# Linear attention and a squared-ReLU layer on one core: the second batch's exp of q by tile and head with its sum on ScalarE, scaling and small additions moved, due dates set anew

## The chip, the core and the metric

The kernel runs on one core of a Trainium2 chip. Its engines are TensorE (PE in the rows), which multiplies matrices, VectorE (DVE), ScalarE (ACT), GpSimd (POOL) and SyncE (SP); SP and ACT also issue DMA transfers. PEld is TensorE's loading of weights. Each engine runs its own list of instructions in order and waits at semaphores. The metric is the device time of one execution in microseconds (us), as the median of several runs.

## The reference

```
def _attn_ref(q, k, v):                       # each (8, 8, 576, 64): batch, heads, sequence, head size
    q_s = exp(q - max(q, axis=-1));  q_s = q_s / (sum(q_s, axis=-1) + 1e-09)
    k_s = exp(k - max(k, axis=2));   k_s = k_s / (sum(k_s, axis=2) + 1e-09)
    kv = einsum('bhsd,bhse->bhde', k_s, v)
    return einsum('bhsd,bhde->bhse', q_s, kv)
x = attn_out.transpose(0, 2, 1, 3).reshape(4608, 512)
r = maximum(x @ w_in, 0.0)                    # w_in (512, 2048)
out = (s * (r * r) + b) @ w_out               # w_out (2048, 512)
```

## The kernel before

**The second layer** takes nearly all of TensorE's time. It goes through 9 blocks of 512 rows of x: one for each batch, with the sequence's first 512 rows, and a last one with the 64 rows left of each batch. In a block there are 16 steps, one for each 128 of the 2048 hidden columns; t counts the steps over all blocks. A step computes `h` (12 matmuls: x and the weights are split into a high and a low part, and three of the four products are summed), takes `r` = relu(h) on ScalarE, makes `gh` and `gl`, the high and low part of s*r*r + b, and adds 12 matmuls to `acc`. There is one PSUM buffer for `h`, so the next h waits for the relu. In the first block a step has two forms: with the square on VectorE, or (every odd t) all on ScalarE but the last subtraction; the second is called the long form here.

**The weights** of the 16 steps are fetched in the first block, and converted there (`conv_w`): on ScalarE two passes (L202, L205) and a cast (L223), on VectorE four passes and a subtraction (L225).

**The attention** works on pairs of heads. A tile u holds two heads, a pair pr two such tiles, so each batch has u = 0 to 3 and pr = 0, 1. For u = 0 to 7 (batches 0 and 1) `q_stream` takes the maximum of q over 64 columns, subtracts it, takes the exp on ScalarE, sums, adds 1e-9, takes the reciprocal, multiplies, turns q with five transposes (`qT`), copies it (`early`), and multiplies it by `kvf` into `xp`, which is cast and split into x. `k_stream` does the same along the sequence with the first batch's k: transpose (`kT`), maximum `km`, exp with its sum, transpose back (`kn`), copy. `heads` computes `kv`; `scales` makes the reciprocal z of k's sums and, with the 0/1 mask `own`, the factors `zr`; `blocks` multiplies kv by them into `kvf`, whose blocks off the diagonal are zero. For the second batch `k_pair` and `kv_second` do this while the first block of the layer runs. Later batches have their own functions, which the change does not touch.

**The order** is made before the program: all this work is written as generators of `Op(engine, cost, due, needs, ...)`, and `Order.run` takes at each point the operation that can start first by its costs; of those within NEAR of each other, the one with the earliest due number. DUE_K, DUE_Q, DUE_V and DUE_W are these numbers for k, q, kv and the first weights; AHEAD sets how many steps ahead a weight tile is due. What comes out is a fixed list for each engine. Where TensorE would wait before the first h, transposes of `ident` into an unused buffer are put in (L948).

**Transfers** are issued by SP in the order of `transfers`, q of the first pair by ACT in `others`.

Of the kernel before, what the change touches and what calls it, by code (L numbers as in the profile page):

```python
# [26 lines left out]
def attention_moe(ctx: ExitStack, tc: tile.TileContext, q, k, v, w_in, w_out, s, b, out):  # L27
# [285 lines left out]
    def blocks(pr, kv, zr):
        kvf = kvfs[pr % 2]
        shape = [P, 2, 2, D]
        nc.vector.tensor_tensor(
            out=kvf, in0=kv.unsqueeze(2).to_broadcast(shape), in1=zr.unsqueeze(3).to_broadcast(shape), op=ALU.mult
        )
        return kvf
# [63 lines left out]
    def kv_second(pr):  # L383
# [4 lines left out]
        yield Op("DVE", 0.5, due)  # L388
        zr = scales(pr, small.tile([P, 2], F32, name=f"z_{pr}", tag="z"), kv[:, :, D])
        yield Op("DVE", 0.4, due, free=["sm"], gives=[f"kvf{pr}"])  # L390
        blocks(pr, kv[:, :, 0:D], zr)

    def kv_stream(pr):
        us = (2 * pr, 2 * pr + 1)
        due = DUE_V[pr]
# [7 lines left out]
        yield Op("DVE", 0.4, due, free=["sm"], gives=[f"kvf{pr}"])  # L403
        blocks(pr, kv, zr)

    def q_stream(u):
# [11 lines left out]
        yield Op("ACT", 0.63, due, take=["qe"], gives=[f"qe{u}"])
        qe = work.tile([P, NT, 2, D], F32, name=f"qe_{u}", tag="qe", bufs=2)
        nc.scalar.activation(qe.rearrange("p n h d -> p h n d"), qt, AF.Exp)  # L420
        yield Op("DVE", 0.73, due)
        qs = small.tile([P, NT, 2], F32, name=f"qs_{u}", tag="qs", bufs=2)
        nc.vector.tensor_reduce(out=qs, in_=qe, axis=AX.X, op=ALU.add)  # L423
        yield Op("DVE", 0.2, due)
        nc.vector.tensor_scalar(qs, qs, 1e-9, None, op0=ALU.add)
# [4 lines left out]
        yield Op("PE", 0.6, due, take=[tag, "qf"], free=["qe"])  # L430
        qT = ps.tile([P, 2, 512], F32, name=f"qT_{u}", tag=tag, bufs=bufs).rearrange("p a b -> p (a b)")
        for n in range(NT):
            nc.tensor.transpose(qT[:, n * P:(n + 1) * P], qe[:, n, :, :].rearrange("p h d -> p (h d)"), ident)
# [565 lines left out]
```

## Time and profile before

| | |
|---|---|
| median of 3 runs | 872.88 us (872.28 to 872.96) |
| the profiled execution | 873.09 us, its span 871.1 us |
| TensorE | 854.6 us busy, 98% of the span |
| VectorE | 576.1 us, 66% |
| ScalarE | 411.9 us, 47% |
| GpSimd | 96.0 us, 11% |
| mean granted clock of TensorE | 0.997 of 2.4 GHz |

The span reaches from the first instruction to the last; the execution's own time is 2.0 us longer. The shares of VectorE and ScalarE are means over stages that differ: in the first block both are far busier than later.

### The profile page before, as it was taken

The page shows a single profiled execution, that of the slowest core. Times are in us where ns is not written, and L with a number is a line of the kernel's source. Part 1 is how long each engine was busy: PE and PEld are TensorE (multiplying, and loading weights), DVE is VectorE, ACT ScalarE, POOL GpSimd, SP SyncE. Part 2 cuts the span into 40 slices and gives each one's busy share as a digit, 9 for nine tenths or more (in the row PEclk, how much of TensorE's full clock was granted, in tenths as well). Part 3 has the DMA queues.
Part 4 walks back from the last instruction along what each step waited for, and adds up shares of the span by engine and source line. Part 5 has one row for each costly group of instructions (what it writes and reads, how often), then busy time and mean ns, then how long its engine had stood idle before and what let it go on. Part 6 is the DMA issues. An engine that isn't in the chain of part 4 may idle for free.

```text
span 871.1 us, 11605 instructions
## 1 busy us (share of the span) xinstructions
PE 854.6 (98%) x4369; PEld 703.6 (81%) x4369; DVE 576.1 (66%) x933; ACT 411.9 (47%) x678; POOL 96.0 (11%) x110
## 2 busy tenths in 40 slices
PE   7899999999999999999999999999999999999997
PEld 6677877888888888888888888888888888888886
DVE  7999997596967778686587758685765332232222
ACT  5898854444554545364345444454444322222222
POOL 1001002020202111120021202030110010000000
PEclk9999999999999999999999999999999999999999
DMA  9977034524343334242433242432311000000001
GB/s 240 320 270 236 13 84 117 130 59 112 121 98 88 83 103 114 89 99 71 130 89 82 89 130 61 109 89 78 81 61 52 25 24 1 1 28 21 1 1 48
DMA packets 110119, 79.44 MB, mean 91 GB/s; under 512 B 60656, under 2 KB 103920, under 8 KB 109936
## 3 DMA queue, kind: packets, MB, share of 16 engines
q1 hardware_dynamic: 108576, 77.60, 32.0%
q10 hardware_dynamic: 1488, 1.12, 0.4%
q8 instruction: 34, 0.56, 0.3%
q14 instruction: 21, 0.17, 0.1%
HBM read 60.29 MB, written 18.40 MB: 90 GB/s over the span
## 4 chain that ended last, share of the span: by engine, by line
PE 86%; issue 6%; DVE 5%; ACT 1%; DMA 1%; POOL 0%; ACTq 0%; DVEq 0%
PE acc L822 41%; PE h L729 41%; PE kv L301 2%; PE xp L679 1%; DVE w L225 1%; DVE low L218 1%; PE xq L679 1%; DMA q<-in_q_dram 1%; DVE low L208 0%; DVE st L213 0%; DVE st L215 0%; POOL k L488 0%; PE xp L443 0%; DVE q L417 0%; DVE qs L423 0%
## 5 line engine op out<-in xcount | busy, mean ns | idle before, releaser
L729 PE MATMUL h<-x,w 128*128 128x512 f32 x1728 | 421.9, 392 | 1.9 <-DVE x L452 0.9
L729 PEld LDWEIGHTS h<-x,w 128*128 128x128 f32 x1728 | 323.5, 188 | 71.5 <-ACT r L773 2.0
L822 PE MATMUL acc<-w,gh 128*128 128x512 f32 x1154 | 357.4, 391 | 0.0
L822 PEld LDWEIGHTS acc<-w,gh 128*128 128x128 f32 x1154 | 214.6, 188 | 44.5 <-ACT last L856 0.4
L788 DVE SCALAR_TENSOR_TENSOR r<-r,sb 128x512 f32<-128x512 f32 x135 | 104.6, 775 | 191.3 <-ACT r L773 190.9
L822 PE MATMUL acc<-w,gl 128*128 128x512 f32 x577 | 224.9, 390 | 0.4 <-DVE gl L785 0.4
L773 ACT ACTIVATE r<-h 128x512 f32<-128x512 f32 x143 | 85.4, 597 | 287.0 <-PE h L729 278.6
L792 DVE SCALAR_TENSOR_TENSOR gl<-r,sb,gh 128x512 fp32r<-128x512 f32 x135 | 107.8, 799 | 53.4 <-ACT gh L790 52.4
L790 ACT ACTIVATE gh<-r,sb 128x512 fp32r<-128x512 f32 x135 | 97.8, 724 | 75.8 <-DVE r L788 75.3
L822 PEld LDWEIGHTS acc<-w,gl 128*128 128x128 f32 x577 | 108.3, 188 | 24.6 <-DVE gl L785 1.6
L578 POOL TENSOR_TENSOR q<-q,qm 128x640 f32<-128x640 f32 x24 | 34.7, 1448 | 174.1 <-DVE qm L576 174.1
L595 POOL TENSOR_TENSOR qe<-qe,qr 128x640 f32<-128x640 f32 x24 | 34.4, 1437 | 58.1 <-DVE qr L591 36.9
L685 ACT COPY y<-xp 64x320 f32<-64x320 f32 x48 | 20.2, 420 | 13.7 <-PE xp L679 13.0
L689 DVE TENSOR_TENSOR y<-xp,y 64x320 f32<-64x320 f32 x48 | 23.5, 489 | 1.5 <-ACT y L685 0.4
L301 PEld LDWEIGHTS kv<-v,k 128*64 128x64 f32 x600 | 18.8, 137 | 6.6 <-issue 4.8
L565 ACT ACTIVATE k<-k 128x640 f32<-128x640 f32 x24 | 17.6, 737 | 13.1 <-DVE k L527 10.3
L659 POOL TENSOR_TENSOR spare<-kvf,spare 128x256 fp32r<-128x256 f32 x12 | 9.7, 808 | 123.1 <-issue 116.1
L301 PE MATMUL kv<-v,k 128*64 128x65 f32 (+1 forms) x600 | 21.0, 224 | 1.3 <-POOL k L488 1.3
L697 DVE TENSOR_TENSOR x<-y,x 128x512 fp32r<-128x512 f32 x24 | 22.3, 931 | 0.0
L599 DVE STREAM_TRANSPOSE q<-qe 128x640 f32<-128x640 f32 x24 | 20.0, 833 | 2.3 <-POOL qe L595 2.3
L616 DVE TENSOR_TENSOR qhl<-qT,qhl 64x640 fp32r<-64x640 f32 x24 | 19.8, 823 | 2.4 <-ACT qhl L611 1.7
L582 ACT ACTIVATE qe<-q 128x640 f32<-128x640 f32 x24 | 18.9, 788 | 5.0 <-POOL q L578 4.8
(126 smaller groups left out, 621.7 us busy)
## 6 DMA issues: line engine op xcount, KB each, us to landing
st<-in_moe_w_in_dram SPq DMA_DIRECT2D x16, 512.0 KB, 8.6
st<-in_moe_w_out_dram SPq DMA_DIRECT2D x16, 512.0 KB, 8.8
out_dram<-o SPq DMA_DIRECT2D x16, 512.0 KB, 2.7
turned<-q SPq DMA_DIRECT2D x24, 320.0 KB, 2.3
qT<-turned SPq DMA_DIRECT2D x48, 160.0 KB, 3.1
q<-in_q_dram SPq DMA_DIRECT2D x14, 512.0 KB, 5.3
k<-in_k_dram SPq DMA_DIRECT2D x14, 512.0 KB, 4.3
v<-in_v_dram SPq DMA_DIRECT2D x56, 128.0 KB, 4.8
```

The lines of the kernel that those rows point to most:

```text
L301: nc.tensor.matmul(kv[h * D:(h + 1) * D, i], kt[:, i, h, n], vt[:, 2 * i + h, n], start=(n == 0), stop=(n == NT - 1))
L578: nc.gpsimd.tensor_tensor(out=qt, in0=qt, in1=bc(qm, [P, 2, NT, D]), op=ALU.subtract)
L595: nc.gpsimd.tensor_tensor(out=qe_, in0=qe_, in1=qr, op=ALU.mult)
L685: nc.scalar.copy(y[half[h], at], parts[h][a][half[1 - h]])
L689: nc.vector.tensor_tensor(out=y[half[h], at], in0=parts[h][a][half[h]], in1=y[half[h], at], op=ALU.add)
L697: nc.vector.tensor_tensor(out=xl, in0=x, in1=xh.bitcast(F32), op=ALU.subtract)
L729: nc.tensor.matmul(hp_, w[:, j, c, :], x[:, c, :], start=(c == 0 and i == 0), stop=(c == NP - 1 and i == 2))
L773: nc.scalar.activation(r, hp_, AF.Relu)
L788: nc.vector.scalar_tensor_tensor(out=r, in0=r, scalar=s_col, in1=r, op0=ALU.mult, op1=ALU.mult)
L790: nc.scalar.activation(gh, r, AF.Identity, bias=b_col)
L792: nc.vector.scalar_tensor_tensor(out=gl, in0=r, scalar=b_col, in1=gh.bitcast(F32), op0=ALU.add, op1=ALU.subtract)
L822: nc.tensor.matmul(acc[blk, j // 2][:, j % 2, c], g[:, js], w_[:, c], start=(f == 0 and i == 0), stop=(f == NFC - 1 and i == 2 and c.stop ...
```

## The change

In `q_stream` the second batch's tiles (u = 4 to 7) no longer subtract the maximum on VectorE and take one exp: the maximum is taken negated, and for each of 2 heads and 5 sequence tiles one exp of 128x64 on ScalarE has it as bias and leaves its sum (`accum_out`). For the first batch (u = 0 to 3) the exp is written into rows of 65 columns whose last one GpSimd sets to 1e-9, so that the sum has it already. `scales` no longer makes `zr`; `blocks` writes the diagonal blocks of `kvf` with four scaled copies on ScalarE, the rest having been set to zero once. The first q load is split in two. Steps of the first block take the long form where t is no multiple of 3. The last output tile is no longer computed and copied in halves. The transfers at the start stand in another order, and the due numbers, AHEAD and NEAR are new.

```diff
-    AHEAD = 1.5
+    AHEAD = 3
-    DUE_Q = (-21.5, -33.5, -5.5, -3.5, 12.5, 8.5, -29, 60.5)
-    DUE_W = -15
+    DUE_Q = (-7, -23, -62.5, -6, 10, 10.5, -23.5, 15)
+    DUE_W = -7
...
-    own = const.tile([P, 2, 2], F32, name="own")
-    nc.gpsimd.memset(own, 0.0)
-    for h in range(2):
-        nc.gpsimd.memset(own[h * D:(h + 1) * D, :, h], 1.0)
+    for t in kvfs:
+        nc.gpsimd.memset(t, 0.0)
...
-        NEAR, HOP, TRIP, RATE = 0.02, 0.15, 3.0, 0.315
+        NEAR, HOP, TRIP, RATE = 0.15, 0.15, 3.0, 0.315
...
-        zr = small.tile([P, 2, 2], F32, name=f"zr_{pr}", tag="zr")
-        nc.vector.tensor_tensor(out=zr, in0=own, in1=z.unsqueeze(2).to_broadcast([P, 2, 2]), op=ALU.mult)
-        return zr
-    def blocks(pr, kv, zr):
-        kvf = kvfs[pr % 2]
-        shape = [P, 2, 2, D]
-        nc.vector.tensor_tensor(
-            out=kvf, in0=kv.unsqueeze(2).to_broadcast(shape), in1=zr.unsqueeze(3).to_broadcast(shape), op=ALU.mult
-        )
-        return kvf
+    def blocks(pr, kv, z):
+        for h in range(2):
+            for i in range(2):
+                nc.scalar.activation(kvfs[pr % 2][half[h], i, h], kv[half[h], i], AF.Copy, scale=z[half[h], i:i + 1])
...
-        nc.vector.tensor_reduce(out=qm, in_=qt, axis=AX.X, op=ALU.max)
+        nc.vector.tensor_reduce(out=qm, in_=qt, axis=AX.X, op=ALU.max, negate=bb > 0)
+        if bb > 0:
+            qe = qs = None
+            for h in range(2):
+                yield Op("ACT", 1.2, due, take=() if h else ["qe"], gives=[f"qe{u}"] if h else ())
...
+                for n in range(NT):
+                    nc.scalar.activation(qe[:, n, h], qt[:, h, n], AF.Exp, bias=qm[:, h, n:n + 1], accum_out=qs[:, n, h:h + 1])
+            yield Op("DVE", 0.31, due)
+            nc.vector.tensor_scalar(qs, qs, 1e-9, None, op0=ALU.add)
+            nc.vector.reciprocal(qs, qs)
+            yield Op("DVE", 0.73, due)
+            nc.vector.tensor_tensor(out=qe, in0=qe, in1=bc(qs, [P, NT, 2, D]), op=ALU.mult)
+            qn = qe
+        else:
...
+            qn = work.tile([P, 2 * NT * (D + 1)], F32, name=f"qe_{u}", tag="qe", bufs=2)
+            qe = qn.rearrange("p (n h e) -> p n h e", h=2, e=D + 1)
+            nc.gpsimd.memset(qe[:, :, :, D:D + 1], 1e-9)
+            nc.scalar.activation(qe[:, :, :, 0:D].rearrange("p n h d -> p h n d"), qt, AF.Exp)
...
-        elif first and (t % 2):
+        elif first and (t % 3):
...
-        parts = half_ if j == NQ - 1 else [whole]
-        for k, c in enumerate(parts):
-            dve = j == 2 or k
...
+        (nc.vector.tensor_copy if j == 2 else nc.scalar.copy)(o, acc[B, j // 2][:, j % 2])
+        for i, (e, eng) in enumerate((("SP", nc.sync), ("ACT", nc.scalar))):
...
         yield from some_k(0, 1)
-        yield from whole(1, 1, "q")
-        yield from whole(0, 2, "v")
         yield from some_k(1, 0)
-        yield from some_k(1, 1)
         yield from fetch(0)
         yield from whole(1, 2, "v")
+        yield from whole(0, 2, "v")
+        yield from some_k(1, 1)
+        yield from whole(1, 1, "q")
...
-        yield Op("ACT", 1.3, -20, gives=["q0 there"], kb=576)
-        load_heads(0, 1, nc.scalar)
+        for i in range(2):
+            yield Op("ACT", 1.2, -20, gives=[f"q0 {i} there"], kb=270)
+            load_heads(0, 1, nc.scalar, 2 * i, 2)
```

How this moves the lists is seen at three places. In SP's queue at the start (`raw` is the tile of the second pair, `st` a fetched weight tile) these rows stood behind the first pair's two loads of k:

```order
L280 DMA raw_91<-in_q_dram 128x4x256
L281 DMA raw_91<-in_q_dram 64x4x64
L280 DMA v_94<-in_v_dram 128x4x256
L281 DMA v_94<-in_v_dram 64x4x64
L274 DMA raw_91<-in_k_dram 128x4x64 x2
L275 DMA raw_91<-in_k_dram 64x2x64
L274 DMA raw_91<-in_k_dram 128x4x64 x2
L275 DMA raw_91<-in_k_dram 64x2x64
L186 DMA st_176<-in_moe_w_in_dram 128x4x256
L188 DMA st_176<-in_moe_w_out_dram 128x1024
```

and now:

```order
L272 DMA raw_89<-in_k_dram 128x4x64 x2
L273 DMA raw_89<-in_k_dram 64x2x64
L184 DMA st_123<-in_moe_w_in_dram 128x4x256
L186 DMA st_123<-in_moe_w_out_dram 128x1024
L278 DMA raw_89<-in_v_dram 128x4x256
L279 DMA raw_89<-in_v_dram 64x4x64
L278 DMA v_92<-in_v_dram 128x4x256
L279 DMA v_92<-in_v_dram 64x4x64
L272 DMA raw_89<-in_k_dram 128x4x64 x2
L273 DMA raw_89<-in_k_dram 64x2x64
L278 DMA raw_89<-in_q_dram 128x4x256
L279 DMA raw_89<-in_q_dram 64x4x64
```

The first weights have moved ahead of v, the last k and the second pair's q, which is now the last of them.

On ScalarE, ahead of the first relu (`r`), stood:

```order
L202 ACTIVATE low_2_438<-st_243 128x1024
L223 CAST w_410<-low_0_342 128x512
L449 CAST x_307<-xp_441 128x512
L243 COPY xleft_457<-xp_441 128x64
L436 COPY early<-qT_448 128x576
L205 ACTIVATE st_243<-st_243 128x1024
L449 CAST x_307<-xp_463 128x512
L243 COPY xleft_457<-xp_463 128x64
L223 CAST w_478<-low_1_413 128x2x512
L773 ACTIVATE r_489<-h_423 128x512
```

and now:

```order
L200 ACTIVATE low_2_446<-st_233 128x1024
L203 ACTIVATE st_233<-st_233 128x1024
L463 CAST x_357<-xp_453 128x512
L241 COPY xleft_472<-xp_453 128x64
L450 COPY early<-qT_464 128x576
L200 ACTIVATE low_3_479<-st_259 128x1024
L463 CAST x_357<-xp_481 128x512
L241 COPY xleft_472<-xp_481 128x64
L221 CAST w_494<-low_1_401 128x2x512
L203 ACTIVATE st_259<-st_259 128x1024
L787 ACTIVATE r_504<-h_459 128x512
```

The cast of the first weights has moved far forward, and both passes over the fourth weight tile (`low_3`, `st_259`) stand ahead of the relu.

On ScalarE, near the end of the first block, the exps of the second batch's q stood as here, one for a tile:

```order
L773 ACTIVATE r_1109<-h_1081 128x512
L790 ACTIVATE gh_1110<-r_1109,sb 128x512
L420 ACTIVATE qe_1131<-q_93 128x2x5x64
L223 CAST w_1151<-low_14_1012 128x2x512
L773 ACTIVATE r_1161<-h_1133 128x512
L487 ACTIVATE k_92<-k_92 128x640
```

and now, the second form of a step around them:

```order
L797 CAST gh_1046<-r_1045 128x512
L419 ACTIVATE qe_1070,qs_1071<-q_91,qm_1057 128x64 x5
L221 CAST w_1084<-low_13_935 128x2x512
L419 ACTIVATE qe_1070,qs_1071<-q_91,qm_1057 128x64 x5
L787 ACTIVATE r_1103<-h_1065 128x512
L419 ACTIVATE qe_1113,qs_1114<-q_91,qm_1086 128x64 x10
L450 COPY early<-qT_1129 128x576
L804 ACTIVATE gh_1104<-r_1103,sb 128x512
```

Ten exps stand for one, and a copy of a turned q and a `gh` stand behind them.

## Rows read from the trace of the kernel before

**Rows 1.** Who waited for whom (TensorE): total us, times, longest us

```profile
PE kv L301 <- POOL k L488: 1.3, 1, 1.3
PE acc L822 <- DVE gl L785: 0.4, 2, 0.2
```

**Rows 2.** TensorE in order of time: start us, us, instructions, idle before

```profile
36.80 4.14 PE L729 MATMUL h<-x,w 128*128 128x512 f32 x10 [0.18 <-DVE w L225]
...
123.20 1.39 PE L301 MATMUL kv<-v,k 128*64 128x65 f32 x40
124.52 0.77 PE L433 MATMUL qT<-ident,qe 128*128 128x128 f32 x5
125.04 0.70 PE L822 MATMUL acc<-w,gh 128*128 128x512 f32 x2
...
135.47 1.24 PE L443 MATMUL xp<-early,kvf 128*128 128x256 f32 x4 [0.73 <-ACT early L436]
136.30 0.87 PE L822 MATMUL acc<-w,gh 128*128 128x512 f32 x2
```

**Rows 3.** The chain that ended last, one piece: start us, us

```profile
154.04 2.72 PE acc L822 x12
```

**Rows 4.** Stretches: their length, busy us by engine, granted clock, DMA

```profile
30.00:35.00 5.00, 3.15 (x12) 1.73 (x10) 5.00 (x9) 3.88 (x7) 0.00 (x0) 1.00 1.04 205
35.00:40.00 5.00, 4.14 (x12) 2.77 (x12) 4.97 (x9) 3.13 (x4) 0.00 (x0) 0.73 1.00 338
38.00:39.00 1.00, 1.00 (x4) 0.81 (x3) 0.97 (x4) 1.00 (x2) 0.00 (x0) 0.50 0.94 361
```

**Rows 5.** SyncE's queue in order of time

```profile
13.25 0.60 SPq L186 DMA_DIRECT2D st<-in_moe_w_in_dram  x1
```

**Rows 6.** ScalarE in order of time, the start

```profile
13.44 0.74 ACT L344 ACTIVATE early<-kT,km 128x576 f32<-128x576 f32 x1 [1.04 <-DVE km L339]
14.08 0.19 ACT L344 ACTIVATION_READ_ACCUMULATOR early<-kT,km 128x1 f32 x1
14.17 0.63 ACT L436 COPY early<-qT 128x576 f32<-128x576 f32 x1
...
18.14 0.68 ACT L202 ACTIVATE low<-st 128x512 int32<-128x512 uint32 x1 [0.54 <-DMA st<-in_moe_w_in_dram]
...
19.44 0.58 ACT L352 COPY raw<-kn 128x512 f32<-128x512 f32 x1
...
20.06 0.58 ACT L449 CAST x<-xp 128x512 fp32r<-128x512 f32 x1
20.54 0.21 ACT L243 COPY xleft<-xp 128x64 f32<-128x64 f32 x1
20.64 0.68 ACT L202 ACTIVATE low<-st 128x512 int32<-128x512 uint32 x1
...
35.23 0.60 ACT L773 ACTIVATE r<-h 128x512 f32<-128x512 f32 x1 [0.35 <-PE h L729]
```

**Rows 7.** ScalarE in order of time, a step of the long form

```profile
40.97 0.60 ACT L773 ACTIVATE r<-h 128x512 f32<-128x512 f32 x1 [0.53 <-PE h L729]
41.47 1.04 ACT L223 CAST w<-low 128x1024 fp32r<-128x1024 f32 x1
42.41 0.64 ACT L779 ACTIVATE r<-r 128x512 f32<-128x512 f32 x1
42.94 1.14 ACT L202 ACTIVATE low<-st 128x1024 int32<-128x1024 uint32 x1
43.98 0.81 ACT L781 ACTIVATE r<-r,sb 128x512 f32<-128x512 f32 x1
```

**Rows 8.** VectorE by line, first block: count, total us, mean ns

```profile
L225 DVE TENSOR_TENSOR w<-low,w 128x1024 fp32r<-128x1024 f32 x15 | 18.1, 1215 | 0.3 <-ACT w L223 0.3
```

**Rows 9.** All engines in order of time, the end

```profile
866.97 0.42 DVE L856 COPY o<-acc 128x256 f32<-128x256 f32 x1 [1.54 <-ACT o L856]
867.21 1.22 ACTq L860 DMA_DIRECT2D out_dram<-o  x2
```

More of the change, by code (lines that the diff above doesn't have):

```diff
@@ L387, in kv_second @@
         heads(kv, by_head(tiles[pr][0]).rearrange("p (u h) n d -> p u h n d", u=2), v_tile(tiles[pr][2]))
[L388 to L391, printed above, removed]
+        yield Op("DVE", 0.33, due)
+        z = small.tile([P, 2], F32, name=f"z_{pr}", tag="z")
+        scales(z, kv[:, :, D])
+        yield Op("ACT", 0.8, due, free=["sm"], gives=[f"kvf{pr}"])
+        blocks(pr, kv[:, :, 0:D], z)
     def kv_stream(pr):
@@ L402, in kv_stream @@
         heads(kv, kt.rearrange("p u n h d -> p u h n d"), vt)
-        yield Op("DVE", 0.4, due, free=["sm"], gives=[f"kvf{pr}"])
-        blocks(pr, kv, zr)
+        yield Op("ACT", 0.8, due, free=["sm"], gives=[f"kvf{pr}"])
+        blocks(pr, kv, z)
     def q_stream(u):
@@ L411, in q_stream @@
         before = [f"kv{NP // 2 - 1}"] + [f"qe{u}" for u in range(NP - 2, NP)]
-        yield Op("DVE", 0.73, due, needs=[f"q{pr} there"])
+        yield Op("DVE", 0.73, due, needs=[f"q{pr} {i} there" if pr == 0 else f"q{pr} there"])
         qt = by_head(tiles[pr][1])[:, 2 * i:2 * i + 2]
         qm = small.tile([P, 2, NT], F32, name=f"qm_{u}", tag="qm")
-        nc.vector.tensor_reduce(out=qm, in_=qt, axis=AX.X, op=ALU.max)
-        yield Op("DVE", 0.73, due)
-        nc.vector.tensor_tensor(out=qt, in0=qt, in1=bc(qm, [P, 2, NT, D]), op=ALU.subtract)
@@ L418, in q_stream @@
[L418 to L425, printed above, removed]
@@ L432, in q_stream @@
         for n in range(NT):
[L433 removed]
+            nc.tensor.transpose(qT[:, n * P:(n + 1) * P], qn[:, n].rearrange("p h d -> p (h d)"), ident)
         yield Op("ACT", 0.53, due, free=[tag])
@@ L801, in step @@
             next(parts)
-            if t == NSTEP - 1 and j == NQ - 1:
-                yield Op("PE", 0.36, t + 0.5, gives=[f"o{t} {NQ}"])
-                next(parts)
     def tile_order(t):
@@ L818, in o_parts @@
             js = slice(j * P, (j + 1) * P)
[L820 to L826 removed]
+            for i, (g, w_) in enumerate(((gh, w[:, 0]), (gh, w[:, 1]), (gl, w[:, 0]))):
+                nc.tensor.matmul(
+                    acc[blk, j // 2][:, j % 2], g[:, js], w_, start=(f == 0 and i == 0), stop=(f == NFC - 1 and i == 2)
+                )
+            yield
     def leave(blk, j):
@@ L843, in leave_last @@
         t = NSTEP - 1
-        whole, half_ = slice(0, DO), (slice(0, DO // 2), slice(DO // 2, DO))
-        o = None
-        parts = half_ if j == NQ - 1 else [whole]
-        for k, c in enumerate(parts):
-            dve = j == 2 or k
-            yield Op("DVE" if dve else "ACT", 0.6 / len(parts), t, needs=[f"o{t} {j + k}"])
-            a = acc[B, j // 2][:, j % 2]
-            if not lasts:
-                lasts.append(work.tile([P, 2 * NT * P], F32, name="last", tag="qhl"))
-            if o is None:
-                o = work.tile([P, DO], F32, name=f"o_{B}_{j}", tag="qe", bufs=2) if j > 1 else lasts[0][:, j * DO:(j + 1) * DO]
-            (nc.vector.tensor_copy if dve else nc.scalar.copy)(o[:, c], a[:, c])
-            for i, (e, eng) in enumerate((("SP", nc.sync), ("ACT", nc.scalar))):
-                yield Op(e, 0.1, t)
-                bb = 2 * j + i
-                eng.dma_start(out[bb * S + TB:(bb + 1) * S, c], o[half[i], c])
+        yield Op("DVE" if j == 2 else "ACT", 0.6, t, needs=[f"o{t} {j}"])
+        if not lasts:
+            lasts.append(work.tile([P, 2 * NT * P], F32, name="last", tag="qhl"))
+        o = work.tile([P, DO], F32, name=f"o_{B}_{j}", tag="qe", bufs=2) if j > 1 else lasts[0][:, j * DO:(j + 1) * DO]
+        (nc.vector.tensor_copy if j == 2 else nc.scalar.copy)(o, acc[B, j // 2][:, j % 2])
+        for i, (e, eng) in enumerate((("SP", nc.sync), ("ACT", nc.scalar))):
+            yield Op(e, 0.1, t)
+            bb = 2 * j + i
+            eng.dma_start(out[bb * S + TB:(bb + 1) * S, :], o[half[i]])
     NU = B * NP
```

43 lines of the change are left out of this document (23 added, 20 removed).

## The prediction, made before the changed kernel had run

> **What bounds the kernel now.** I read the waits first, then TensorE's own order of time, then ScalarE's. From about 41 us to the end TensorE is never long without work. In the waits after the start only two places count: 1.3 us in front of a kv product, where k's zeroed rows came late [rows 1], and 0.7 us in front of the product at 135.47 us [rows 2]; with two waits of 0.2 us they are 2.4 us. So a second can be won or lost only in the start (up to the second tile's h product), in these stalls of the first block, and in the tail.
>
> In the start the table by stretches shows VectorE busy 5.00 of 5 us from 30 to 35 us and 4.97 of the next 5, ScalarE 3.88 and 3.13, TensorE 3.15 and 4.14 [rows 4]. VectorE sets the pace there. TensorE, with 3.15 of 5 us, waits for the products' copies, and then its granted clock falls: 1.00 until 35 us, 0.50 (1.2 GHz) from 38 to 39, 0.73 as the mean from 35 to 40 [rows 4]. It shows in the second tile's h: ten matmuls took 4.14 us [rows 2], where twelve take 2.72 later [rows 3], so ten should take 2.27 plus the last one's 0.16 of drain. The fall costs 1.7 us. The second tile's h ends at 36.80 + 4.14 = 40.94 us.
>
> **The start in the changed order.** Work leaves VectorE: four small additions of 1e-9, the scaling by `own`, and both `kvf` products. It arrives on ScalarE, which was not full. What counts is whether ScalarE is now the later one. I take the stretch of its queue from the first conversion of w0 to the first `relu` of h. Before, it began when w0's transfer landed, at 18.14 us, and the relu started at 35.23 [rows 6]: 17.1 us, waits included. The order of the changed kernel, counted over the whole stretch, has everything that stood in it and in addition:
> - two exps of k with their sums: 14.17 - 13.44 = 0.73 each [rows 6], 1.46
> - one copy of a turned q, 0.63 less the 0.1 by which instructions overlap: 0.53 [rows 6]
> - one pair of copies of a turned k, 19.44 to about 20.06: 0.62 [rows 6]
> - one exp of q, near the 0.64 that k's exp alone takes to the next start [rows 6]: 0.65
> - eight scaled copies for the two `kvf`. No such instruction stands in the trace. Nearest are the 128x64 copy, whose successor starts 0.10 later, and its own duration of 0.21 [rows 6]. With a scale read from memory I take 0.17: 1.36 (ends 0.8 and 1.7)
> - both conversions of the fourth weight tile, which AHEAD = 3 puts ahead of the relu: 42.94 to 43.98 is 1.04 [rows 7], twice: 2.08
>
> That is 6.7. The stretch begins earlier: sixteen issues stood ahead of w0's in SP's queue, which came to it at 13.25 us [rows 5]. Nine stand there now: 9/16 of 13.25 is 7.5, and 18.14 - 13.25 = 4.9 to landing gives 12.4. SP's issues of the k groups are slower than the mean, so 13.0 (12.3 to 14). The relu then starts at 13.0 + 17.1 + 6.7 = 36.8. Two more copies now wait for transposes of k that were not in the stretch; 0.2 for that: 37.0. The relu frees the one h buffer 0.6 later, so the second tile's h runs from 37.65. It needs 12 x 0.227 = 2.72, hence 40.4 at full clock. Before, two of the twelve were done at 36.3 and ten began at 36.80. TensorE's wait of over a microsecond ahead of it remains, so I let the clock fall as before: 42.1. Against 40.94 that is +1.2, and two transposes of the k maxima that stood ahead of this point now come later, +0.2. **Start: +1.4**; +0.4 to +2.4 with the ends above; 1.7 less if the clock stays up.
>
> The Trainium skill, in "TensorE: Matmul & The Clock Gate", section "Part 1: The HAM clock gate", says that the monitor's window runs free of the kernel, so the same kernel meets its clock changes at different points from run to run. One trace cannot show that; by that rule the 1.7 us is not owed in each run.
>
> Hidden: the split of the first q load adds two DMA issues to ScalarE's queue, while it waits for VectorE to subtract the maximum anyway. If that cover were gone it would cost those two issues, about 1 us. GpSimd's added memsets lie in a queue that has nothing else to do then. The last start load is now q of the second pair, in the place of v, early enough by the same pace of issues.
>
> **The first block's end.** Each q tile of the second batch has ten exps of 128x64 with an accumulator read where one exp stood, and VectorE's subtraction and sum go. Price of a pair: a copy of 64 columns takes 0.21 [rows 6], one pass over 512 takes 0.60 [rows 7], so 0.87 ns a column; k's exp, 0.74 for 576 [rows 6], becomes 0.30 for 64, of which the next instruction overlaps 0.10; the read adds 0.09 (14.08 to 14.17) [rows 6]. 0.29; I take **0.30**. Lower end 0.19 (the 0.10 of the plain copy, and the read), upper end 0.49 (nothing overlaps).
>
> Now ScalarE is full there. In the changed order I add up its queue from the relu of the twelfth tile (t = 11) to the cast of the sixteenth weight tile: 4 relus 2.0, three long steps' squares 1.6, scalings 2.1 and casts 1.65, one gh 0.6 (paces from start to start, the scaling's 0.81 less 0.1 [rows 7]; the cast like the relu), 30 pairs 9.0, weights 3 x 0.94 + 3 x 1.04 = 5.9 [rows 7], three copies of qT 1.6, three casts of x with their leftovers 1.75, two exps of k 1.3, four scaled copies 0.7: 28.2. Add 0.2 until the relu starts, VectorE's subtraction of 1.2 [rows 8] less the 0.46 in which TensorE's first two matmuls need no such rest, and 0.1 to hand over: 29.3. TensorE needs in the same stretch 7.75 x 2.72 = 21.1 [rows 3], three qT at 0.52, one kv at 1.32, three xp at 0.83 [rows 2] and 0.4 of small transposes: 26.9. So it stalls by **2.4 us**, in pieces: ahead of an xp, of a weight tile's rest, of qT. The old stalls were 2.4 as well. **Block: 0.** Each 0.01 us on a pair is 0.3 us here.
>
> The skill's "ScalarE: Activation LUTs", section "What ACT_TABLE_LOAD costs", has a dearer price: 280 ns and 0.833 ns a column with a bias read from memory, 93 ns of it overlapped, which with the read's row makes an estimate of 0.33. By it the stall would be 3.3 and the time 0.9 us later.
>
> **The tail.** The last output tile was copied in two halves, but ScalarE's half began only when all six matmuls were done, and VectorE's waited for ScalarE's half (1.54 us, until 866.97), so the second pair of issues began at 867.21 + 0.6 = 867.8, and the span ends at 871.1 [rows 9]. One whole copy of 0.6 ends at about 867.2 and both queues issue at once: 0.6 earlier, with transfers twice as large. **Tail: -0.4** (0 to -0.7). Six pieces of 256 columns or three of 512 are the same to TensorE.
>
> **Sum.** 1.4 + 0 - 0.4 = +1.0 us. The profiled execution took 873.09, its span 871.1; it would be 874.1 with a span of 872.1. The median of the runs is 0.2 lower, hence **873.9**. What a measurement can tell here is 0.2%, 1.75 us.
>
> **Rivals.**
> - *The clock does not fall in the dense part*, by another phase or a filled gap: 873.9 - 1.7 = 872.2. For it: the fall covers one short stretch. Against it: TensorE's gaps before the second h are no shorter. 0.2.
> - *ScalarE cannot take the exps at 0.30* (the other side). Its place is the queue above; at 0.33 a pair it gives 874.8, at 0.38 the stall is 4.8 and the time 876.3. From 0.33 on, with the 0.9 us it adds, it ends slower by my bound. For it: each exp depends on a bias column and each read on its exp; upper end 0.49. Against: the accumulator row shows the overlap. 0.2.
> - *The pairs are cheap*, 0.24 or less, so that the stall falls to 0.6 (872.1), and the clock stays up too: 870.4, faster. 0.15.
> - *The change does nothing* because TensorE is full: that holds for everything after the first block, and is in the sum.
>
> **How the numbers follow.** The forecast has 0.45. With its own spread of 1 us about a fifth of it lies over 874.6. Faster comes from the third case and a little of the first: 0.17. Slower: most of the second case and that fifth, and late transfers (a w1 or q that lands 1 us later delays the start as much): 0.3. The rest, 0.53, is the same. The range from 871.4 to 876.2 leaves out about a tenth on each side.
>
> **What would show it.** After: the first relu of h near 37 us and not at 35; ScalarE, not VectorE, full from 25 to 37 us; the exps of 64 columns near 0.30 with their read; waits of TensorE near 2.4 us between the products of t = 11 and t = 15, on ScalarE's copies and VectorE's tiles behind it; clock at 0.50 somewhere from 37 to 43 us; last issues near 867.2 plus the shift. I am wrong if ScalarE has idle time in that stretch of the block, or if the relu comes at 35.

## The result and the profile after

The changed kernel took 874.73 us as the median of 10 runs (874.02 to 876.20), the kernel before 872.81 (872.03 to 873.19): a ratio of 1.0025, 95% interval 1.0017 to 1.0033. That is 1.9 us slower; the forecast was 873.9, range 871.4 to 876.2. The interval of the ratio reaches to both sides of the prediction's bound of 0.2%, so it doesn't tell for certain whether the change is slower by that bound. The profiled execution took 874.54 us, its span 872.7, against 871.1 before.

In the rows of the changed kernel L743 is h, L787 its relu, L831 acc, L419 the new exps, L312 the scaled copies for `kvf`, L200, L203 and L221 ScalarE's part of a weight tile, L223 VectorE's last, L450 the copy of a turned q, L457 xp, L463 and L466 the cast and the leftover of x.

First the stretches of the start: length, then busy time (instructions) of TensorE, its weight loads, VectorE, ScalarE, GpSimd; granted clock, DMA share, GB/s. They answer to [rows 4].

```profile
30.00:35.00 5.00, 4.34 (x26) 3.24 (x24) 4.07 (x7) 4.97 (x10) 0.00 (x0) 1.00 1.08 354
35.00:40.00 5.00, 3.47 (x11) 2.03 (x12) 4.93 (x7) 4.72 (x8) 0.00 (x0) 1.00 1.12 335
```

ScalarE is now full from 30 to 35 us, where it had been busy 3.88, and the clock does not fall in the start. ScalarE in order of time, beside [rows 6]:

```profile
13.81 0.66 ACT L200 ACTIVATE low<-st 128x512 int32<-128x512 uint32 x1 [1.82 <-DMA st<-in_moe_w_in_dram]
...
23.02 1.02 ACT L312 ACTIVATE kvf<-kv,z 64x64 f32<-64x64 f32 x4
...
36.44 0.59 ACT L463 CAST x<-xp 128x512 fp32r<-128x512 f32 x1 [0.27 <-PE xp L457]
...
37.97 1.17 ACT L203 ACTIVATE st<-st 128x1024 f32<-128x1024 f32 x1
39.03 0.60 ACT L787 ACTIVATE r<-h 128x512 f32<-128x512 f32 x1
```

TensorE, beside [rows 2]:

```profile
37.92 0.73 PE L743 MATMUL h<-x,w 128*128 128x512 f32 x2 [0.34 <-DVE x L466]
39.68 3.04 PE L743 MATMUL h<-x,w 128*128 128x512 f32 x12 [1.03 <-ACT r L787]
42.56 0.62 PE L831 MATMUL acc<-w,gh 128*128 128x512 f32 x2
...
110.66 1.24 PE L457 MATMUL xp<-early,kvf 128*128 128x256 f32 x4 [0.80 <-ACT early L450]
...
122.66 0.74 PE L447 MATMUL qT<-ident,qe 128*128 128x128 f32 x5 [1.52 <-DVE x L466]
```

The first relu comes at 39.03, not near 37; the second h then runs its twelve matmuls at the full clock, and acc begins at 42.56, against 40.91 before (its row stands below). Later TensorE waits 0.80 and 1.52 us in the block's end, and 0.6 in two pieces ahead of other qT: 2.9 where the forecast had 2.4. What stands ahead of that x on ScalarE is a group of exps:

```profile
117.17 0.34 ACT L419 ACTIVATE qe<-q,qm 128x64 f32<-128x64 f32 x1
117.42 0.19 ACT L419 ACTIVATION_READ_ACCUMULATOR qe<-q,qm 128x1 f32 x1
117.51 0.34 ACT L419 ACTIVATE qe<-q,qm 128x64 f32<-128x64 f32 x1
...
120.50 0.56 ACT L463 CAST x<-xp 128x512 fp32r<-128x512 f32 x1
```

Ten pairs fill 117.17 to 120.50: 0.333 us each, and the cast of x stands behind them. Their tile's sum, reciprocal and product and then the leftover of x (121.82) follow on VectorE. The end, beside [rows 9]:

```profile
867.62 0.40 PE L831 MATMUL acc<-w,gl 128*128 128x512 f32 x1
868.11 0.59 ACT L857 COPY o<-acc 128x512 f32<-128x512 f32 x1 [0.27 <-PE acc L831]
868.72 0.47 SPq L861 DMA_DIRECT2D out_dram<-o  x1
868.76 0.56 ACTq L861 DMA_DIRECT2D out_dram<-o  x1
```

**Where the 1.6 us between the two spans lie.** Up to the first acc +1.65 (40.91 to 42.56). From there to the relu of t = 17, with the same products in between, -0.31: it came at 143.19 before and at 144.53 after, 102.28 and 101.97 us later. From there to the end of the last matmul +0.21 (866.47 before, 867.62 + 0.40 = 868.02 after). From that to the span's end +0.05 (4.63 and 4.68). The sum is 1.60. The rows behind this, of the kernel before:

```profile
40.91 0.71 PE L822 MATMUL acc<-w,gh 128*128 128x512 f32 x2
...
143.19 0.60 ACT L773 ACTIVATE r<-h 128x512 f32<-128x512 f32 x1 [1.57 <-PE h L729]
...
866.19 0.28 PE L822 MATMUL acc<-w,gl 128*128 128x256 f32 x1
```

and of the changed kernel:

```profile
144.53 0.60 ACT L787 ACTIVATE r<-h 128x512 f32<-128x512 f32 x1 [1.70 <-PE h L743]
```

### The profile page after: what moved, and what is told of

It is laid out like the page before. It is cut to its first block, busy times and chain, and to the rows that moved or that the text cites. A ratio compares the mean times of both kernels' runs of the same rounds, so it can differ in the third digit from the quotient of the medians.

```text
span 872.7 us, 11730 instructions
## 1 busy us (share of the span) xinstructions
PE 855.0 (98%) x4383; PEld 704.3 (81%) x4383; DVE 569.6 (65%) x910; ACT 428.6 (49%) x774; POOL 92.5 (11%) x113
## 4 chain that ended last, share of the span: by engine, by line
PE 91%; ACT 5%; DMA 1%; SPq 1%; issue 1%; DVE 0%; ACTq 0%; DVEq 0%
PE acc L831 44%; PE h L743 44%; PE kv L299 2%; ACT qe L419 2%; PE xp L693 1%; PE xq L693 1%; DMA raw<-in_q_dram 1%; DMA k<-in_k_dram 1%; ACT st L203 0%; SPq L272 0%; PE xp L457 0%; ACT low L200 0%; SPq L273 0%; ACT early L450 0%; ACT r L787 0%
## 5 line engine op out<-in xcount | busy, mean ns | idle before, releaser
L743 PE MATMUL h<-x,w 128*128 128x512 f32 x1728 | 422.0, 391 | 1.5 <-ACT r L787 1.0
L743 PEld LDWEIGHTS h<-x,w 128*128 128x128 f32 x1728 | 322.2, 188 | 70.0 <-ACT r L787 1.5
L831 PE MATMUL acc<-w,gh 128*128 128x512 f32 x1152 | 357.1, 391 | 0.0
L831 PEld LDWEIGHTS acc<-w,gh 128*128 128x128 f32 x1152 | 214.6, 188 | 45.1 <-ACT last L857 0.4
L802 DVE SCALAR_TENSOR_TENSOR r<-r,sb 128x512 f32<-128x512 f32 x133 | 107.1, 805 | 195.3 <-ACT r L787 194.2
L831 PE MATMUL acc<-w,gl 128*128 128x512 f32 x576 | 224.3, 389 | 0.0
L787 ACT ACTIVATE r<-h 128x512 f32<-128x512 f32 x143 | 85.5, 598 | 270.6 <-PE h L743 267.0
L806 DVE SCALAR_TENSOR_TENSOR gl<-r,sb,gh 128x512 fp32r<-128x512 f32 x133 | 104.7, 787 | 53.7 <-ACT gh L804 52.1
L831 PEld LDWEIGHTS acc<-w,gl 128*128 128x128 f32 x576 | 108.1, 188 | 22.9 <-DVE gl L799 0.2
L699 ACT COPY y<-xp 64x320 f32<-64x320 f32 x48 | 20.3, 422 | 25.2 <-PE xp L693 24.9
L703 DVE TENSOR_TENSOR y<-xq,y 64x256 f32<-64x256 f32 x48 | 20.3, 422 | 0.9
L630 DVE TENSOR_TENSOR spare<-qT,spare 64x640 fp32r<-64x640 f32 x24 | 20.1, 838 | 0.7
L707 ACT CAST x<-y 128x512 fp32r<-128x512 f32 x24 | 14.8, 617 | 11.2 <-DVE y L703 11.2
```

The lines of the kernel that those rows point to most:

```text
L630: nc.vector.tensor_tensor(out=t[half[1 - h], h], in0=qT[half[h]], in1=t[half[h], h].bitcast(F32), op=ALU.subtract)
L699: nc.scalar.copy(y[half[h], at], parts[h][a][half[1 - h]])
L703: nc.vector.tensor_tensor(out=y[half[h], at], in0=parts[h][a][half[h]], in1=y[half[h], at], op=ALU.add)
L743: nc.tensor.matmul(hp_, w[:, j, c, :], x[:, c, :], start=(c == 0 and i == 0), stop=(c == NP - 1 and i == 2))
L787: nc.scalar.activation(r, hp_, AF.Relu)
L802: nc.vector.scalar_tensor_tensor(out=r, in0=r, scalar=s_col, in1=r, op0=ALU.mult, op1=ALU.mult)
```

## The experiments

All medians are of runs that went in turns with the kernel before on one chip, and the ratios are to those runs; its medians there were 872.72 (the first four experiments), 872.96 (the clock, and order or code alone), 873.02 (one part alone) and 872.91 (the q tiles). "List kept" means that every other instruction stays in its place. A mean clock is that of a whole run: it tells that the clock fell, and not where.

### The exps of the second batch undone in the changed kernel

```diff
-  nc.vector.tensor_reduce(out=qm, in_=qt, axis=AX.X, op=ALU.max, negate=bb > 0)
+  nc.vector.tensor_reduce(out=qm, in_=qt, axis=AX.X, op=ALU.max)
...
+  nc.vector.tensor_tensor(out=qt, in0=qt, in1=bc(qm, [P, 2, NT, D]), op=ALU.subtract)
...
-  for n in range(NT):
-      nc.scalar.activation(qe[:, n, h], qt[:, h, n], AF.Exp, bias=..., accum_out=...)
+  if h:
+      nc.scalar.activation(qe.rearrange("p n h d -> p h n d"), qt, AF.Exp)
...
+  nc.vector.tensor_reduce(out=qs, in_=qe, axis=AX.X, op=ALU.add)
```

Expected: 

> The changed kernel with its list of operations kept, but the second batch's exps of q as before: VectorE subtracts the maximum right after it is found, one exp stands in the place of the last five, and VectorE sums. ScalarE loses 10 x 0.33 - 0.65 = 2.65 us a tile, 10.6 for the four; VectorE gains 2 x 0.8 = 1.6 us a tile, 6.4 for the four. Theory 1 (the forecast's: in the first block the exps only exchange VectorE's stall for one of ScalarE): the start is untouched, acc of the first step begins near 42.6, the block again stalls by 2 to 4 us, now on VectorE's tiles; 874.7, within 0.9. Theory 2 (the exps are what the change loses): the stalls of 2.9 us between the products of t = 12 and t = 15 go without any in their place, and the time is 872.0 to 873.0. A time of 876 or more says that the exps on ScalarE are a gain which the start hides.

Measured: 877.93 us, ratio 1.0062 (1.0050 to 1.0075), 3.2 more than the changed kernel. In its trace the granted clock is 0.70 as the mean from 15 to 20 us, 0.66 from 40 to 45 and 0.91 from 100 to 120; the two runs with a mean clock of 0.998 took 877.26 and 877.39, 2.7 more than the changed kernel's runs at 0.997 and over. Who TensorE waited for, 36 to 160 us (total us, times, longest):

```profile
PE qT L448 <- DVE qe L425: 1.9, 1, 1.9
PE qT L448 <- DVE x L467: 1.8, 1, 1.8
```

Neither theory of the loss holds, and the time lies where the expectation read a gain, at 876 or more: in this list the exps on ScalarE save about 3 us. Without them TensorE waits for VectorE's qe and x.

### kvf back on VectorE in the changed kernel

```diff
-  for h in range(2):
-      for i in range(2):
-          nc.scalar.activation(kvfs[pr % 2][half[h], i, h], kv[half[h], i], AF.Copy, scale=z[half[h], i:i + 1])
...
+  nc.vector.tensor_tensor(out=zr, in0=own, in1=z.unsqueeze(2).to_broadcast([P, 2, 2]), op=ALU.mult)
...
+  nc.vector.tensor_tensor(out=kvfs[pr % 2], in0=kv..., in1=zr..., op=ALU.mult)
```

Expected: 

> The changed kernel with its list kept, but kvf written by VectorE as before (0.16 for the factors and 0.41 for the product, twice in the start) in the place of eight scaled copies on ScalarE, which took 0.25 each, 2.0 us in the start. Theory 1 (ScalarE's queue from the conversion of the first weights to the first relu sets the start, as the forecast summed it): the relu comes about 2 us earlier, near 37.0 in the place of 39.03, and the time falls by 1.5 to 2.0, to near 873.0. Theory 2 (VectorE's chain, x's subtraction and the second weight tile's, sets it as much): the first h still ends near 38.6 and the second tile's rest near 39.6, so the relu comes at most 0.4 earlier and the time is 874.3 to 875.2, since VectorE has 1.1 us more to do.

Measured: 875.77, ratio 1.0036 (1.0022 to 1.0050). ScalarE has 2.0 us less to do in the start, and the first relu comes later, not earlier:

```profile
30.64 0.74 ACT L439 ACTIVATE qe<-raw 128x640 f32<-128x640 f32 x1 [0.53 <-DVE raw L433]
...
39.79 0.62 ACT L792 ACTIVATE r<-h 128x512 f32<-128x512 f32 x1
```

The exp of q (29.88 in the changed kernel) now waits for VectorE's subtraction, which stands behind the two `kvf` products. ScalarE's queue is full, but what fills it waits in turns for VectorE. This is theory 2's mechanism, but past its figures: it had the relu up to 0.4 earlier and at most 875.2.

### One pass over the fourth weight tile moved behind the first relu

```diff
+        if f == 3:
+            later.append(lambda: nc.scalar.activation(lo.bitcast(F32), hi.bitcast(F32), AF.Abs))
...
             nc.scalar.activation(r, hp_, AF.Relu)
+            while later:
+                later.pop()()
```

Expected: 

> The changed kernel with its list kept, but the second of the two ScalarE passes over the fourth weight tile, 1.06 us, stands behind the first relu and not ahead of it. Theory 1 (the queue's sum counts): the relu comes 1.06 earlier and so does the second tile's h, 873.7. Theory 2 (the pass only fills a wait): the first h ends at 38.65 whatever ScalarE does, since its last quarter waits for VectorE's x, and the second weight tile's rest is there at 39.60, so the relu comes 0.4 earlier, the second tile's h less than 0.1, and the time is unchanged, 874.7 within 0.5.

Measured: 874.67, ratio 1.0023 (1.0015 to 1.0032): no change. The relu is at 38.66, 0.37 earlier, as theory 2 had it, and waits for h:

```profile
38.66 0.60 ACT L792 ACTIVATE r<-h 128x512 f32<-128x512 f32 x1 [0.60 <-PE h L748]
...
41.24 0.75 ACT L811 ACTIVATE gh<-r,sb 128x512 fp32r<-128x512 f32 x1
```

The second h came 0.37 earlier too, which theory 2 had not, but `gh`, behind the moved pass, came 0.34 later (41.24 for 40.90), and the gain was gone.

### The old tail in the changed kernel

```diff
+  for c in [slice(i * DO // 2, (i + 1) * DO // 2) for i in range(2)] if t == NSTEP - 1 and j == NQ - 1 else [slice(0, DO)]:
...
+  parts = half_ if j == NQ - 1 else [whole]
```

Expected: 

> The changed kernel with the old tail: the last output tile in six pieces of 256 columns, copied in halves by ScalarE and VectorE, four issues. Theory 1 (the forecast: the whole copy saves 0.4): 0.4 slower than the changed kernel, 875.1, and the span ends 5.0 to 5.1 us after the last matmul's start. Theory 2 (the span ends a fixed time after the last issues, and the whole copy's 0.59 and the larger transfers eat what one pair of issues saves): no difference, 874.7 within 0.3; from the last matmul's start to the span's end 4.6 to 5.1 either way.

Measured: 876.03 (874.63 to 876.95), ratio 1.0033 (1.0020 to 1.0046), but in its profiled execution this isn't the tail. There the clock fell in the second h (granted clock 0.50, 1.2 GHz, from 41 to 43 us), and once before, from 15 to 20 us (0.66 as the mean):

```profile
39.78 4.61 PE L743 MATMUL h<-x,w 128*128 128x512 f32 x12 [1.02 <-ACT r L787]
44.23 0.63 PE L836 MATMUL acc<-w,gh 128*128 128x512 f32 x2
```

```profile
15.00:20.00 5.00, 4.00 (x21) 4.00 (x22) 4.18 (x11) 4.58 (x11) 0.00 (x0) 0.66 1.21 276
41.00:43.00 2.00, 2.00 (x6) 1.52 (x6) 2.00 (x3) 2.00 (x3) 0.00 (x0) 0.50 0.73 149
```

The first fall moved the first relu by 0.10 only (39.13); the second is the rest. acc begins at 44.23, 1.67 after the changed kernel's 42.56, and the spans (874.3 and 872.7) differ by no more. From the relu of t = 142, the last in one piece, to the span's end it took 15.84 us, the changed kernel 15.94, the kernel before 15.88. In the traces the tail is worth 0.1 or less either way: theory 2. The other four runs have no trace. One of them took 876.95 at a mean clock of 0.998, so not all of the spread is the clock's.

### The clock kept up in the start of both kernels

```diff
+    def fill(n):
+        t = ps.tile([P, 512], F32, name="fill", tag="sm", bufs=1)
+        for _ in range(n):
+            nc.tensor.transpose(t[:, 0:P], ident, ident)
...
+            if (t, c) in ((0, 3), (1, 0)):
+                fill(...)   # before: 7 and 6, and 7 ahead of the fourth xp; changed: 2 and 8
             hp_ = next(parts)
```

Expected of the kernel before: 

> The kernel before, with TensorE's gaps ahead of the second tile's h filled: 7 transposes of the identity ahead of the fourth xp, 7 ahead of the first h's last quarter, 6 ahead of the second h, into the small PSUM buffer, where the kernel before waits 0.91, 0.94 and 0.69 us. Nothing else waits for them. If the clock then stays at 2.4 GHz in the start, theory 1 (the forecast: the fall costs the kernel before 1.7 us) gives 871.1. Theory 2 (VectorE, full from 30 to 72 us, takes the gain back: TensorE only waits longer for gl and in front of the kv product at 68 us, where GpSimd's zeroing comes late) gives 872.8, unchanged within 0.4, with a wait of 2 to 3 us in the place of 1.34 in front of that product.

Measured: 872.89, ratio 1.0000 (0.9992 to 1.0009). TensorE in order of time:

```profile
36.96 2.57 PE L739 MATMUL h<-x,w 128*128 128x512 f32 x10 [0.19 <-DVE w L225]
...
39.51 0.71 PE L834 MATMUL acc<-w,gh 128*128 128x512 f32 x2
...
43.52 2.56 PE L739 MATMUL h<-x,w 128*128 128x512 f32 x10 [0.34 <-DVE w L225]
...
47.24 0.50 PE L834 MATMUL acc<-w,gl 128*128 128x512 f32 x1 [0.44 <-DVE gl L797]
```

The ten matmuls take 2.57 us where they took 4.14 [rows 2], and acc begins 1.4 earlier. Of that, 0.3 is left by 47.24 (47.55 before): TensorE waits for VectorE's weights and gl. The kernel before's row there:

```profile
47.55 0.50 PE L822 MATMUL acc<-w,gl 128*128 128x512 f32 x1 [0.23 <-DVE gl L785]
```

So in these traces the fall cost the kernel before 0.3 us; the medians, known to 0.8 us, show no difference. The kernel before's own runs beside the experiments agree: the 19 at a mean clock of 0.999 or 1.000 have a median of 872.54, the other 38 one that is 0.4 higher. This is theory 2's mechanism, though the wait at the kv product grew to 1.4 only, since gl and w had taken the rest.

Expected of the changed kernel: 

> The changed kernel with the same gaps filled: 2 transposes ahead of the first h's last quarter (a wait of 0.34) and 8 ahead of the second h (1.03). Its runs at a mean clock of 0.995 took 875.9 and 876.2, the others 874.0 to 875.0. Theory 1 (the clock's fall in the second h costs the changed kernel its full 1.7 us, and comes in a part of the runs): no run over 875.3, median 874.4. Theory 2 (the spread has another cause): as before, median 874.7 with single runs near 876.

Measured: 874.45 (874.09 to 875.04, 11 runs), ratio 1.0017 (1.0008 to 1.0026): theory 1. Two of the changed kernel's ten runs had taken 876.2 and 875.9, and none of these does. Two of ten against none of eleven would be weak alone; the trace with the old tail shows the price itself. That a fall costs the changed kernel 1.6 us to the end fits its stretches (the same columns), set against those of the filled kernel before:

```profile
45.00:60.00 15.00, 15.00 (x67) 12.40 (x67) 14.90 (x20) 14.76 (x19) 0.00 (x0) 1.00 1.07 380
60.00:80.00 20.00, 20.00 (x90) 16.56 (x89) 19.67 (x26) 19.06 (x24) 0.00 (x0) 1.00 0.52 183
```

```profile
45.00:60.00 15.00, 14.40 (x61) 10.91 (x60) 15.00 (x20) 14.59 (x19) 0.00 (x0) 1.00 1.06 379
60.00:80.00 20.00, 18.62 (x116) 15.13 (x115) 19.41 (x29) 18.63 (x24) 3.62 (x2) 1.00 0.50 139
```

In the first pair, the changed kernel's, TensorE never waits: what it loses in the start stays lost. In the second it waits 0.6 and 1.4 us, and these waits swallow it.

### The order alone, and the code alone

The first gives the code before the changed kernel's due numbers (all four lists: DUE_K and DUE_V are new too), AHEAD, NEAR, `t % 3` and order of transfers; the second the reverse.

Expected of the order alone: 

> The code before with the changed kernel's due numbers, AHEAD, NEAR, form of the steps and order of transfers; the exps, kvf, the additions and the tail as before. Theory 1 (the forecast: the loss is the start's, where w3's conversion and the transfers' order lengthen the way, and the exps are neutral): about half of the loss, 873.5, with VectorE full from 20 to 40 us and the first relu at 37 to 38. Theory 2 (the exps on ScalarE are a gain, which the new order gives back and more): 876 to 878, with VectorE's stalls in the first block's end. Theory 3 (the order is better and the code loses): 872 or less.

Expected of the code alone: 

> The changed code (exps, kvf on ScalarE, additions, whole tail, first q in two loads) with the due numbers, AHEAD, NEAR, form of the steps and transfers of before. Theory 1 (the forecast: exps neutral, kvf on ScalarE costs the start up to 2 us): 873.5 to 874.5. Theory 2 (the exps are a gain of 3 us wherever VectorE is full at the block's end, and the loss is the new order's): 870 to 872. Theory 3 (old numbers fit the new code badly): over 875, with a stall of its own that the trace names.

Measured: 879.82, ratio 1.0078 (1.0064 to 1.0091), and 882.96, ratio 1.0114 (1.0099 to 1.0128). The waits of TensorE, 30 to 145 us, of the order alone and then the largest two of the code alone:

```profile
PE h L729 <- DVE w L225: 2.4, 1, 2.4
PE h L729 <- ACT r L773: 1.6, 1, 1.6
```

```profile
PE xp L457 <- ACT early L450: 3.0, 3, 1.3
PE h L743 <- ACT w L221: 2.7, 1, 2.7
```

Alone they cost 6.9 and 10.0 us, together 1.9. In both traces the clock also fell, in the second h among other places (mean clock 0.993); but the fastest runs, at 0.997 and 0.996, still took 877.97 and 881.01. Old work under new numbers has its first relu at 42.30, and VectorE is late with a weight tile at 124 us, the block's end, where theory 2 put its stall; the median lies over that theory's 878 us. New work under old numbers makes ScalarE late: theory 3. A sum over the parts, which stood behind all these sizes, doesn't hold.

### One part alone in the kernel before, its list kept

The edits are those of the first two experiments the other way round: the second batch's exps by tile and head, and `kvf` by four scaled copies.

Expected of the exps: 

> The kernel before, its list kept, with one part of the change alone: the second batch's exps of q by tile and head on ScalarE with the maximum as bias and the sum from the accumulator. VectorE loses 4 x 1.6 = 6.4 us, ScalarE gains 4 x 2.65 = 10.6. Theory 1 (the forecast's: stalls of VectorE only turn into stalls of ScalarE, the block stays the same): 872 to 874. Theory 2 (a list made for one short exp has a relu or a cast of x right behind it, so that each group of ten holds up TensorE by up to 2.65): 875 to 879, with TensorE waiting for relus, turned q and x behind the exps. Theory 3 (VectorE, 19.9 of 20 us busy from 80 to 120, is what holds the kernel back): 871 or less.

Expected of kvf: 

> The kernel before, its list kept, with kvf written by four scaled copies on ScalarE in the place of VectorE's factors and product. In the start ScalarE, 5.00 and 4.97 of 5 us busy from 20 to 30 us, gains 2.0 us, VectorE loses 1.15. Theory 1 (the forecast's sum over ScalarE's queue): the first relu comes 1 to 2 us later, 36.2 to 37.2, and the time is 873.5 to 874.5. Theory 2 (the second h waits for VectorE's weight tile, and VectorE has less to do): the relu moves by less than 0.5 and the time is 872.3 to 873.2.

Measured: 877.57, ratio 1.0059 (1.0045 to 1.0073), theory 2; and 875.65, ratio 1.0032 (1.0020 to 1.0043), 1.2 over the end of theory 1's range. TensorE with the exps alone:

```profile
127.72 0.74 PE L439 MATMUL qT<-ident,qe 128*128 128x128 f32 x5 [2.04 <-DVE qe L435]
136.21 2.35 PE L735 MATMUL h<-x,w 128*128 128x512 f32 x9 [1.17 <-ACT r L779]
```

The second wait is for a relu that stands behind ten exps (132.24 to 135.57). With `kvf` alone the first relu is at 36.48 for 35.23, inside theory 1's 36.2 to 37.2, and TensorE's wait for a copy of a turned q is 1.81 us at 29.82. Its two runs at a mean clock of 0.999 took 874.81 and 874.99, nearer to theory 1's 874.5. Half of its loss comes only after t = 14 (1.2 late there, 2.4 at t = 142). Of that, 0.7 lies between the relus of t = 14 and 15, where TensorE now waits for `kvf` itself; the rest I did not follow:

```profile
129.01 1.24 PE L438 MATMUL xp<-early,kvf 128*128 128x256 f32 x4 [0.43 <-ACT kvf L313]
```

### One or two q tiles of four in the old form

The edit of the first experiment, for the third tile of the second batch, and for the second and the third.

Expected of one: 

> The changed kernel, its list kept, with the third of the four q tiles of the second batch in the old form (subtraction and sum on VectorE, one exp), the other three by tile and head. ScalarE loses 2.65 us from 117 to 120.5, ahead of the cast of x on whose leftover TensorE waits 1.52 us at 122.66; VectorE gains 1.6 there, where it has about 1.5 us of idle time from 120 to 130. Theory 1 (ScalarE's queue is what stalls TensorE at the block's end, so the exps' price sets those waits): the wait of 1.52 goes, 873.2. Theory 2 (all four exps pay or none: each tile's way over VectorE costs as much as it frees, as the kernel with all four undone was 3 us slower): 875 to 876.

Expected of two: 

> The same with the second and the third q tile in the old form. The second's exps stand ahead of the copy of the turned q on which xp waits 0.80 us at 110.66. Theory 1: both waits go, 0.80 and 1.52, and the time is 872.4. Theory 2: VectorE, with 1.7 us free from 100 to 120, cannot take 3.2 more, and the time is above the one with the third tile alone: 874 to 876.

Measured: 876.75 (1.0041, 1.0029 to 1.0053) and 875.87 (1.0043, 1.0030 to 1.0056). Both lie with theory 2 and not with theory 1, though not in its figures: one tile took more than its 876, and two took no more than one, where it said more. No mixture beats the changed kernel. VectorE with the third tile in the old form:

```profile
118.28 1.22 DVE L223 TENSOR_TENSOR w<-low,w 128x1024 fp32r<-128x1024 f32 x1
119.41 1.54 DVE L500 TENSOR_TENSOR k<-k,mb 128x640 f32<-128x640 f32 x2
120.87 0.81 DVE L426 TENSOR_REDUCE qs<-qe 128x10 f32<-128x640 f32 x1
...
122.30 0.83 DVE L430 TENSOR_TENSOR qe<-qe,qs 128x640 f32<-128x640 f32 x1
123.04 0.68 DVE L472 TENSOR_TENSOR x<-xp,x 128x512 fp32r<-128x512 f32 x1
```

ScalarE cast x at 118.70 there, 1.8 earlier; its leftover now stands behind the sum in VectorE's queue and comes at 123.04, where the changed kernel has it at 121.82. The runs with a mean clock of 0.995 took 876.8 and 877.0, and 877.4 and 879.2 with two tiles; those at 0.998 and 0.999 took 875.6, and 875.3 to 875.9. In the trace with two old tiles, where the clock stayed up, the wait of 0.80 is gone as expected, waits for VectorE took its place, and the span is 873.9.

## Why the prediction was right, and where its steps were not

**The sum** was +1.0 on the span, measured +1.6, by way of two errors in the start that cancel. That the start's number came out is luck.

**Start, +1.4: measured +1.65.** (a) The stretch from w0's conversion to the first relu was forecast at 17.1 + 6.7 + 0.2 = 24.0 us from 13.0 on. It took 25.2 from 13.81 on. w0 landed 0.8 late; four scaled copies took 1.02, 0.25 each for my 0.17, 0.7 in all; 0.5 is not placed. The relu at 39.03 is 2.0 off. (b) "The fall costs 1.7 us", and "I let the clock fall as before": in the profiled execution it didn't fall. So 40.4 + 1.7 became 42.56 by another way. The prediction had argued that TensorE's gaps ahead of the second h are no shorter. The one just ahead of it isn't (1.03, where the kernel before waited 0.69, and not over a microsecond), but from 30 to 35 us TensorE was busy 4.34 of 5 and not 3.15.

**The steps that failed.** In the sum these are the relu's time, 2.0 us too early, and the fall, which did not come. A third is the reading of the kernel before: VectorE sets the pace, I wrote, and then priced the fall on TensorE at its full 1.7 us. The filled kernel before shows 0.3, and its own runs 0.4. This price didn't move the sum, which compares the two at the first acc. In the changed kernel, whose TensorE never waits from 45 to 80 us, the price is right: in the trace with the old tail it is 1.67 at acc and 1.6 in the span. The condition of the rival without a fall held in the profiled execution; its 872.2 lacked (a)'s 2.0 us.

The sum over ScalarE's queue in (a) is also less than it seemed. It gave the relu's time to 2 us, but neither of two items tried could be bought back: 2.0 us less of it, put on VectorE, made the relu 0.76 later, and 1.06 less made no difference to the end. The way to the second h goes back and forth between ScalarE and VectorE, both over 4.7 of 5 us busy from 35 to 40. Which edit would shorten it stays open.

**Block, 0: measured -0.3.** The pair's price was mis-sized, 0.30 for 0.333. That is the estimate from the Trainium skill's "ScalarE: Activation LUTs", section "What ACT_TABLE_LOAD costs", which the trace bears out. Named stalls are 2.9, between my 2.4 and the 3.3 of that price. They are 0.5 longer than in the kernel before, yet the stretch is 0.3 shorter, so about 0.8 was won in pieces that the list of waits doesn't name; which these are stays open. That an exchange of stalls nets to nothing holds between these two lists; within either list undoing or adding the exps alone costs 3 to 5 us.

**Tail, -0.4: measured +0.05.** The last issues do come 0.6 earlier against the shift, but the span ends 4.0 us after them, not 3.3. With the old tail in the changed kernel it is 3.2 again (871.1 to 874.3), so the later end goes with the whole tile, whose last transfers are twice as large; no run took size and number of transfers apart.

**The rest**, +0.21 from t = 17 on, was not forecast and no run tests it. By the relus it comes in the next blocks: they are 1.34 us apart at t = 20 (159.51 and 160.85), 1.56 at t = 64 (414.94 and 416.50) and at t = 142 (855.22 and 856.78).

**The rivals.** ScalarE takes the exps at 0.33, the second rival's price, and 874.8 was its time; but the way there is another. 874.8 against the measured 874.73 is therefore luck. Against the forecast the parts are +0.25 in the start, -0.31 in the block, +0.21 behind it and +0.45 in the tail, 0.6 in all; the dearer exps made no loss between these two lists. Cheap pairs are excluded.

## What to carry to other kernels

Before a stall or a slower clock is priced, look for the next place where the engine waits: what is lost ahead of such a wait is given back there, and a kernel without later waits pays it in full. A part of a change that a planner has fitted to its order can't be priced by undoing it alone: here a part undone or done alone cost 1 to 10 us more, or changed nothing, while the whole cost 1.9. A full queue is a bound only if its items don't wait for another engine's; take one item out and see whether the last one moves.

## What the runs showed of the hardware

**The clock's fall is a matter of the run.** The same changed kernel ran with a mean clock of 0.999 in 872.2 to 873.0 us of span, and with 0.995 in 874.0 and 874.4; the four runs between took 872.4 to 873.2. In the trace of it with the old tail TensorE stood at 1.2 GHz in the second h after a wait of 1.02 us; in its own trace it stayed at 2.4 after one of 1.03. That agrees with the Trainium skill's "TensorE: Matmul & The Clock Gate", section "Part 1: The HAM clock gate", by which the same kernel meets these changes at different points; with eight transposes in that gap none of eleven runs took more than 875.04. What a fall costs is a matter of its place: in the trace with the old tail the one from 15 to 20 us moved the first relu by 0.10, the one in the second h acc by 1.6 more.

**Two zeroings by GpSimd took 3.6 us instead of 0.4.** In the kernel before (here with the filled start) they lie under six passes of one input on VectorE, and end 0.3 after the last of them; alone, at 115.06, one takes 0.20:

```profile
64.39 3.62 POOL L498 MEMSET k<- 64x128 f32 x2 [46.68 <-issue]
115.06 0.20 POOL L498 MEMSET k<- 64x128 f32 x1 [47.05 <-ACT k L497]
```

```profile
63.95 1.39 DVE L208 TENSOR_SCALAR low<-st 128x1024 uint16<-128x1024 uint16 x2
65.23 1.31 DVE L213 TENSOR_SCALAR st<-st 128x1024 f32<-128x1024 f32 x2
66.44 1.28 DVE L215 TENSOR_SCALAR st<-st 128x1024 uint32<-128x1024 uint32 x2
```

This is the wait of 1.3 us at the kv product [rows 1], which looked like late work on GpSimd and, by these rows, comes of VectorE's passes. The Trainium skill's "SBUF — State Buffer", section "Who interferes with whom", says that such a pass of VectorE can hold a pair of ports that it shares with GpSimd, and that the other is blocked meanwhile; the rows agree, over six passes in a row. But in the changed kernel two such zeroings began at 93.57 us beside three passes, took 1.39 and ended inside the third, so a row of passes need not hold them to its end. No run here took the passes away, and the cause of the 3.6 us is argued.
